# A hand-written schedule in another order behind its 199th step (routing attention, then a SiLU layer, one core)

## The chip, the cores and the metric

The kernel runs on one core of a Trainium2 chip. The metric is the device time of one execution in microseconds (us), lower is better. Three runs of the kernel before gave 294.0, 295.02 and 587.43 us, so their median is 295.02; the third is twice the other two and says nothing about the kernel's work. A fourth execution, taken with the profiler, gave 293.75 us.

The engines are named as in the profile: PE multiplies matrices (PEld is its loading of weights), ACT is the scalar engine, DVE the vector engine, POOL the third engine for elementwise work, and SP only issues transfers. Each takes its instructions strictly in the order in which they stand in its own queue, and waits at the first one whose inputs are not there.

## The reference

Shapes: q, k and v are [4, 8, 768, 64] (batch, heads, sequence, head width), there are 16 centroids per head, w_in is 512 x 2048 and w_out 2048 x 512. All are float32.

```
q_assign = argmax(q_n . c_n);  k_assign = argmax(k_n . c_n)        # cluster of each row, 16 per head
scores = where(q_assign == k_assign, (q . k^T) / sqrt(64), -1e9)
attn = softmax(scores);  x = attn . v                              # -> [3072, 512]
h = x @ w_in;  out = (h * sigmoid(h)) @ w_out
```

## The kernel before

The kernel has no loop over its work. A table of 1628 words, `plan`, is read from front to back, and each word emits one step through `step(op, n, eng, banks)`. The letters say what the step does, the number says which head, unit or tile, a letter behind the point chooses the engine of a copy (A is ACT, D is DVE, P is POOL), and digits there choose PSUM banks. The pools hand out buffers in the order of the steps, and the semaphores follow from that. So the table alone sets the order on all five queues.

There are 32 heads in all (4 batches of 8). A head n passes through these steps:

- `r` loads q and k (L92, on SP); `hi` and `lo` split float32 into two float16 halves (L103/L105/L107 by engine, and L112 on DVE). The `hl` tile that they fill is one of four, so `hi` also waits until an earlier head's tile has been read.
- `ht` turns the tile by a DMA transpose into `ab` (L121, on SP). Heads 0 to 7 do this on PE instead.
- `l` multiplies `ab` with the centroids on PE (L159, 12 matmuls of 32 columns). `ls`, `mx`, `ge` (DVE) make the cluster's one-hot rows of it.
- The one-hot rows are written into partitions 64 to 79 of `ab`, for the mask is part of the score's matmul. Heads 8 to 15: `cm` on PE, `ce` (L237 on ACT or L239 on DVE), and a transfer on SP (L240). Heads 16 to 31: `cs` on POOL (L204, L205), `cx`, a DMA transpose on SP (L213), and `cv`, a transfer on POOL's queue (L217).
- `qk` makes two score tiles of 384 columns on PE (L336) in one of two double banks, `ex` their exponentials on ACT (L341), `pv` multiplies them with v (36 matmuls of 65 columns, L353), `nm` normalises (DVE, L363, L365). `pt` and `pe` (PE, then a copy) or `xd` (L392, a DMA transpose on SP) turn the result into `xt`. `vl` loads v, `v` casts it (L277 on ACT, L279 on DVE or POOL).

The layer behind it: for batches 0 and 1 `a` and `e` multiply with w_in (L401), `t` is the tanh (ACT, L413) and `g` the gate (DVE, L416). For batches 2 and 3 `y` (L467), `u` and `s` do the same with fewer products. The second matrix is `b` (L498) for three row tiles, and `m` (L559) with its sums `S` (DVE, L572) and copies `z`, `o` (L587, L581, L590) for the rest. The weights come in through twelve transfers on POOL's queue: `w0` to `w7` w_in (L608, 256 KB each), `w8` to `w11` w_out (L611, 512 KB each). Each stands behind a copy of one element (`pace`, L604) that reads the newest exponential tile, which holds it back until that exponential is done.

Every transfer of SP stands in one queue, whatever it is for, and an SP transfer that must wait holds all behind it.

Of the kernel before, what the change touches and what calls it, by code (L numbers as in the profile page):

```python
# [29 lines left out]
def kernel(  # L30
# [655 lines left out]
    def step(op, n, eng, banks):  # L686
# [138 lines left out]
        ex19 qk21 xL1.2 ex20 w8 xM1 ex21 qk22 qk23 pt2.0 ex22 ex23 xm1 px3.1 qk24 pe0.D lo8 xg1 xc1 py3 qk25 ex24 qk26  # L825
        pe2.D a1.0 xe1.A nm3 pt3.1 pe3.D a0.2 ex25 ex26 qk27 ex27 e1 e4.1 e0 t4 g4 vl10 qk28 t0 g0 qk29 ex28 e6.3 t6
        g6 ex29 vl11.P e3.1 t3 w9 t1 e5.2 qk30 ex30 w11 g3 lo9 r13 vl8 qk31 t5 pv4.3 qk32 ex31 nm4 e8.1 g1 g5 qk33 ht8
        lo10 hi11.P e14.0 ex32 ex33 t14 g14 qk34 t8 ex34 qk35 e11.2 e13.3 ht10 g8 wc4 wc5 t11 g11 r12 ex35 t13 g13
        qk36 ex36 e10.1 e15.0 qk37 pt4.2 qk38 e2.3 t10 ex37 ex38 lo11 pe4.D ht9 r14 pv5.2 g10 t15 nm5 qk39 qk40 t2
        ex39 ex40 e7.1 e12.2 t12 ht11 g15 qk41 ex41 t7 g2 r15 wc6 e9.0 qk44 g7 t9 g9 pv6.3 nm6 wc0 wc8 ex44 qk42 ex42  # L830
        b0.1 pt5.0 v11.P l8.3 ls8 mx8 hi13.P ge8 lo13 qk43 qk45 pe5.A b4.0 ex43 qk47 wc12 wc1 cm8.3 b1 ex45 g12 ce8.A
        qk46 ex46 l10.3 b5 ls10 mx10 l9.2 ls9 ht13 mx9 b6 b7 od1 ex47 ge9 cm9.3 hi12.A lo12 ce9.A bo1 pv7.2 nm7 hi14.A
        b2 pt6.3 pt7.0 pe7.A ht12 r16 ge10 lo14 l11.2 ls11 ht14 mx11 b3 cm10.0 bo0 ce10.D pe6.A e25.3 t25 qk50 ex50
        ge11 g25 qk48 hi15.D e27.2 cm11.1 t27 g27 ce11.A e20.0 t20 lo15 ex48 qk49 g20 e17.3 t17 l12.1 hi16.P ex49 vl13
        e23.2 qk52 ls12 mx12 l13.0 ls13 g17 ex52 t23 g23 vl9 e31.1 t31 od2 qk75 e28.0 ex75 v8.P t28 g31 e18.3 t18 mx13
        qk51 ex51 qk53 v10.A e24.2 t24 ge12 g18 g28 l14.1 ls14 mx14 e22.3 qk59 ge13 ex53 cm12.0 ex59 ht15 r18 e29.1
        t29 qk54 ex54 ce12.D g24 cm13.0 ce13.D g29 t22 g22 qk55 ex55 lo16 ge14 e19.2 t19 g19 v9.A e16.0 e30.1 t16 g16
        qk57 r17 t30 qk56 e21.3 t21 m1.2 ex56 g30 wc15 wc13 r19 g21 ht16 l15.0 ls15 ex57 S3 pv8.1 vl17 qk58 nm8 cm14.3
# [15 lines left out]
        ex101 vl23 e63.0 S21 qk124 ex124 e53.3 qk105 t53 g53 e51.2 t51 v18.A g51 pv16.1 nm16 e55.3 cs23 ex105 cv22
        qk128 t63 ex128 g63 v19.A m22.2 qk130 ex130 vl21 S22 m21.1 z20.A v23.P o20 qk109 ex109 qk110 ex110 vl28 v22.A
        m26 qk108 ex108 l24.0 hi27.D lo27 ht27 cx23 pv17.2 z21.D ls24 qk113 mx24 qk112 t55 v21.P l26.0 g55 ex113 m25
        nm17 ls26 mx26 r28 cv23 ex112 xd16 xd17 qk111 ex111 qk131 ex131 e57.3 t57 e52.2 v28.A z22.D S24 qk126 ex126
        m27.0 qk127 g57 pv18.3 o23 r30 hi25.D lo25 nm18 qk115 ht25 ex127 qk116 m24 o22 ex115 ex116 qk114 ex114 xd18
# [69 lines left out]
```

## Time and profile before

| | |
|---|---|
| three runs | 294.0, 295.02, 587.43 us |
| the profiled execution | 293.75 us, of which the span of its instructions is 292.0 us |
| PE | 284.4 us busy, 97% |
| ACT | 244.5 us, 84% |
| DVE | 228.3 us, 78% |
| POOL | 66.7 us, 23% |
| granted TensorE clock | full in every slice |

Times in the profile are microseconds from the span's start. A row of instructions gives the engine, the line of the kernel, the operation, output and input names, shapes, how many, and then the busy time and the mean of one in nanoseconds; behind it stands how long the engine was idle before them and who ended that. A row of the timeline gives start, duration, engine, line and, in brackets, idle time and its releaser; rows of equal neighbours are merged, so their duration can hold a gap. Matmuls are pipelined: a row's matmuls start closer together than the mean of one says.

### The profile page before, as it was taken

How to read it: one execution, taken by the hardware profiler on the slowest of the kernel's cores; microseconds unless marked ns; L12 is line 12 of the kernel's file. 1: busy time of each engine (PE TensorE's matmuls, PEld its weight loads, DVE VectorE, ACT ScalarE, POOL GpSimd, SP SyncE). 2: the span in 40 equal slices, each digit the busy share in tenths (PEclk: the TensorE clock that was granted, in tenths of full speed). 3: DMA queues.
4: the chain of work that ended last, by engine and by line, in shares of the span. 5: the costliest groups of instructions: out<-in, count | busy, mean ns of one | idle time of the engine just before them, and what ended most of it. 6: DMA issues, size and time to landing. Idle time of an engine off the chain costs nothing.

```text
span 292.0 us, 8452 instructions
## 1 busy us (share of the span) xinstructions
PE 284.4 (97%) x3356; PEld 208.4 (71%) x3356; DVE 228.3 (78%) x498; ACT 244.5 (84%) x427; POOL 66.7 (23%) x114
## 2 busy tenths in 40 slices
PE   7899999999999999999999999999999999999995
PEld 3767766756678886776777788765687878656884
DVE  5898949699999999878788899888944623897662
ACT  5898999976989999988999998879899989486631
POOL 2654905110400015552232042111220000000000
PEclk9999999999999999999999999999999999999999
DMA  7999999999898888999778796392000222210032
GB/s 209 288 274 237 188 182 198 206 229 210 217 221 178 194 193 177 202 199 231 190 118 193 193 190 123 77 245 85 18 24 2 88 43 76 74 38 2 2 124 92
DMA packets 75750, 44.01 MB, mean 151 GB/s; under 512 B 53872, under 2 KB 72080, under 8 KB 75712
## 3 DMA queue, kind: packets, MB, share of 16 engines
q1 hardware_dynamic: 71584, 38.01, 55.9%
q0 software_dynamic: 3840, 5.18, 10.5%
q8 instruction: 26, 0.43, 0.6%
q10 hardware_dynamic: 288, 0.30, 0.4%
q14 instruction: 12, 0.10, 0.1%
HBM read 27.30 MB, written 6.29 MB: 115 GB/s over the span
## 4 chain that ended last, share of the span: by engine, by line
PE 87%; DVE 4%; DMA 3%; ACT 3%; issue 1%; SPq 0%; DVEq 0%; ACTq 0%
PE pS L336 20%; PE xb L559 18%; PE ph L401 14%; PE pO L353 11%; PE gd L467 5%; PE psN L159 4%; PE yb L559 3%; PE gx L467 3%; PE po L498 2%; PE gy L467 2%; DMA xt<-xn 2%; DMA raw<-in_q_dram 1%; PE wb L559 1%; ACT P L341 1%; DVE hl L112 1%
## 5 line engine op out<-in xcount | busy, mean ns | idle before, releaser
L341 ACT ACTIVATE P<-pS 128x768 f16<-128x768 f32 x192 | 149.7, 816 | 10.1 <-PE pS L336 8.4
L336 PE MATMUL pS<-ab 128*128 128x384 f16 x384 | 86.8, 326 | 0.3 <-ACT P L341 0.2
L401 PE MATMUL ph<-xt,win_s 128*128 128x384 f16 x256 | 49.7, 326 | 0.5 <-DMA xt<-xn 0.4
L336 PEld LDWEIGHTS <-ab 128*128 128x128 f16 x384 | 33.8, 98 | 15.1 <-issue 1.8
L353 PEld LDWEIGHTS <-P 128*128 128x128 f16 x1152 | 39.7, 97 | 3.8 <-DVE cd L239 0.4
L416 DVE SCALAR_TENSOR_TENSOR gt<-tn,ph 128x384 f16<-128x384 f32 x64 | 33.6, 548 | 10.6 <-ACT tn L413 10.3
L353 PE MATMUL pO<-vt,P 128*128 128x65 f16 x1152 | 41.3, 193 | 0.0
L559 PEld LDWEIGHTS <-gt 128*128 128x128 f16 x352 | 34.2, 98 | 7.2
L401 PEld LDWEIGHTS <-win_s 128*128 128x128 f16 x256 | 24.4, 98 | 16.0 <-issue 0.9
L413 ACT ACTIVATE tn<-ph 128x384 f32<-128x384 f32 x64 | 30.6, 507 | 3.8 <-PE ph L401 3.2
L112 DVE SCALAR_TENSOR_TENSOR hl<-raw,hl 128x768 f16<-128x768 f32 (+3 forms) x35 | 31.8, 912 | 0.2
L559 PEld LDWEIGHTS <-s 128*128 128x128 f16 x264 | 25.7, 98 | 5.3
L105 POOL TENSOR_SCALAR hl<-raw 128x768 f16<-128x768 f32 (+1 forms) x10 | 20.2, 2016 | 28.2 <-DMA raw<-in_k_dram 15.1
L559 PE MATMUL xb<-wout_s,gt 128*128 128x256 f16 x176 | 22.6, 273 | 0.0
L159 PEld LDWEIGHTS <-ab 128*128 128x128 f16 x496 | 18.0, 97 | 4.0 <-DVE ab L146 0.4
L559 PE MATMUL xb<-wc,s 128*128 128x256 f16 x160 | 20.7, 273 | 0.0
L204 POOL TENSOR_SCALAR od<-od 128x96 f16<-128x96 f16 x16 | 9.6, 599 | 48.3 <-DVE od L197 45.6
L581 ACT ACTIVATE ot<-xb 128x256 f32<-128x256 f32 x33 | 12.8, 387 | 8.6 <-PE xb L559 8.4
L159 PE MATMUL psN<-stk,ab 128*128 128x32 f16 (+1 forms) x496 | 19.1, 186 | 0.0
L572 DVE TENSOR_TENSOR s<-gt 128x1024 f16<-128x1024 f16 x22 | 15.3, 694 | 4.7 <-PE xb L559 3.8
L365 DVE TENSOR_TENSOR xn<-pO,zr 128x384 f16<-128x384 f32 x32 | 17.8, 558 | 1.1
L467 PEld LDWEIGHTS <-win_s 128*128 128x128 f16 x128 | 12.3, 98 | 8.5 <-issue 0.8
(128 smaller groups left out, 412.5 us busy)
## 6 DMA issues: line engine op xcount, KB each, us to landing
raw<-in_k_dram SPq DMA_DIRECT2D x31, 192.0 KB, 3.7
vn<-in_v_dram SPq DMA_DIRECT2D x31, 192.0 KB, 3.7
raw<-in_q_dram SPq DMA_DIRECT2D x24, 192.0 KB, 3.7
out_dram<-ot SPq DMA_DIRECT2D x18, 256.0 KB, 2.7
win_s<-in_moe_w_in_dram POOLq DMA_DIRECT2D x8, 256.0 KB, 6.9
wout_s<-in_moe_w_out_dram POOLq DMA_DIRECT2D x4, 512.0 KB, 9.2
out_dram<-ot SPq DMA_DIRECT2D x12, 128.0 KB, 1.7
raw<-in_q_dram SPq DMA_DIRECT2D x2, 384.0 KB, 5.9
```

Of the source, the lines that this page charges most:

```text
L105: nc.gpsimd.tensor_scalar(out=o, in0=i, scalar1=QS, scalar2=None, op0=ALU.mult)
L112: nc.vector.scalar_tensor_tensor(out=hl[:, s, 1, :], in0=raws[job.name][:, s, :], scalar=QS, in1=hl[:, s, 0, :], op0=ALU.mult, op1=ALU.sub ...
L159: nc.tensor.matmul(L[:, n % 2, :, n // 2], ab[:, i, :], stk[:, job.groups[i // 3][0], x : x + w], start=(x == 0), stop=(x + w == 2 * HC),)
L336: nc.tensor.matmul(pS[:, e, 0:HALF], abs_[kj.name][:, kn, :], rhs, start=True, stop=True)
L341: nc.scalar.activation(out=P, in_=pst.pop(u)[:, :, 0:HALF], func=AF.Exp, bias=0.0, scale=ESC)
L353: nc.tensor.matmul(o[:, (2 * t + h) * VW : (2 * t + h + 1) * VW], Ps[i + h, c, j // 2][:, j % 2, ts(t, 128)], vtb[(i + h) % 13][:, j, 0:VW ...
L365: nc.vector.tensor_tensor(out=xn, in0=ov[:, :, 0:D], in1=zr.unsqueeze(2).to_broadcast([128, 2 * NM, D]), op=ALU.mult)
L401: nc.tensor.matmul(ph[:, 0:HALF], win_s[:, r, ts(fb, 128)], xts[b, c][:, r, :], start=(r == 0), stop=(r == NR - 1))
L413: nc.scalar.activation(out=tn, in_=phs[b, c, fb][:, 0:HALF], func=AF.Tanh, bias=0.0, scale=0.5)
L416: nc.vector.scalar_tensor_tensor(out=gt[:, fb, NM * c : NM * c + NM, :].rearrange("p t n -> p (t n)"), in0=tns.pop((b, c, fb)), scalar=1.0 ...
L467: nc.tensor.matmul(o[:, 0:HALF], w[:, r, :], x[:, r, :], start=(s in (7, 1) and r == 0), stop=(r == 1), skip_group_check=True)
L559: nc.tensor.matmul(o, self.lhs(l, f), self.rhs(r, f), start=(f == 0 and opens), stop=(f == HB - 1), skip_group_check=True)
```

## The change

The table keeps its 1628 steps, and each step keeps what it computes. The first 199 words stay. From the 200th on the words stand in another order, many with other bank digits, and some copies with another engine letter. Among the first 450 steps the transfers keep the order that they had among themselves. The engine letters move this work, counted over the whole program: on ACT three fewer `hi`, seven fewer casts of v and one fewer copy to `xt`, six more copies in the products' mixes (L481) and one more of the cluster rows; on DVE six fewer copies in the mixes (L479) and one fewer of the cluster rows, three more casts, one more `hi` and one more copy to `xt`; on POOL two more `hi` and four more casts.

```diff
@@ -822,74 +822,74 @@
-        ex19 qk21 xL1.2 ex20 w8 xM1 ex21 qk22 qk23 pt2.0 ex22 ex23 xm1 px3.1 qk24 pe0.D lo8 xg1 xc1 py3 qk25 ex24 qk26
...
+        ex19 qk21 ex20 xL1.1 qk23 xM1 xm1 pt2.2 pe2.D ex21 qk22 px3.0 xg1 ex23 ex22 qk27 ex27 xc1 qk25 ex25 lo9 py3
...
```

Three places follow. The first is on PE, at the centroid product of head 8 (the first `psN` of 32 columns; `ab_1221` there and `ab_1293` now are that head's transposed tile). The rows of before, of which repeats are left out:

```order
L498 LDWEIGHTS gt_95
L498 MATMUL po_1463<-wout_s_67,gt_95 128x512
L374 LDWEIGHTS xn_1360
L374 MATMUL px_1468<-ident_84,xn_1360 128x128
L159 LDWEIGHTS ab_1221
L159 MATMUL psN_1473<-stk_68,ab_1221 128x32
```

And the rows now:

```order
L353 LDWEIGHTS P_1217
L353 MATMUL pO_1303<-vt3_73,P_1217 128x65
L159 LDWEIGHTS ab_1293
L159 MATMUL psN_1344<-stk_68,ab_1293 128x32
L336 LDWEIGHTS ab_426
L336 MATMUL pS_1357<-ab_877,ab_426 128x384
```

It stood as PE's row 1564 and stands as row 1422 now: 71 matmuls that were ahead of it are behind it. By kind they are 16 of L401, 4 of L498, 36 of L353, 12 of L336 and 3 of L374.

The second place is POOL around the last three of w_out's transfers. Before, from the 43rd row of its queue:

```order
L743 MEMSET od_92 128x256
L604 COPY pace<-P 1x1
L611 DMA wout_s<-in_moe_w_out_dram 128x4x512
L271 DMA vn<-in_v_dram 128x384
L604 COPY pace<-P 1x1
L611 DMA wout_s<-in_moe_w_out_dram 128x4x512
L604 COPY pace<-P 1x1
L611 DMA wout_s<-in_moe_w_out_dram 128x4x512
L105 TENSOR_SCALAR hl<-raw 128x12x64
L279 CAST vt_81<-vn 128x6x64
```

And now:

```order
L743 MEMSET od_92 128x256
L604 COPY pace<-P 1x1
L611 DMA wout_s<-in_moe_w_out_dram 128x4x512
L105 TENSOR_SCALAR hl<-raw 128x12x64
L271 DMA vn<-in_v_dram 128x384
L604 COPY pace<-P 1x1
L611 DMA wout_s<-in_moe_w_out_dram 128x4x512
L604 COPY pace<-P 1x1
L611 DMA wout_s<-in_moe_w_out_dram 128x4x512
L743 MEMSET od_94 128x256
```

The three are w8, w9 and w11. Head 11's `hi` moved ahead of v's load and of w9 and w11. Each `pace` copy reads another exponential than before: in the table w8 stands behind ex24 (it stood behind ex20), w9 behind ex26 (ex29, but with more of PE's work ahead of it now) and w11 behind ex33 (ex30).

The third place is DVE, where the second halves of heads 8 and 9 are made (`hl_853` is head 8's tile, `hl_940` head 9's; `cd` are the cluster rows of the pair x1). Before:

```order
L112 SCALAR_TENSOR_TENSOR hl_853<-raw_213,hl_853 128x12x64
L197 TENSOR_TENSOR om0_89<-psN_965,mxn_1010 128x192
L385 COPY xt_942<-px_1002 128x384
L363 RECIPROCAL zr_1073<-pO_1012 128x6
L365 TENSOR_TENSOR xn_1075<-pO_1012,zr_1073 128x384
L385 COPY xt_942<-px_1077 128x384
L416 SCALAR_TENSOR_TENSOR gt_95<-tn_1102,ph_1096 128x384
```

And now:

```order
L197 TENSOR_TENSOR om0_89<-psN_967,mxn_995 128x192
L112 SCALAR_TENSOR_TENSOR hl_940<-raw_589,hl_940 128x12x64
L239 TENSOR_SCALAR cd_1069<-psN_967 96x256
L385 COPY xt_942<-px_826 128x384
L363 RECIPROCAL zr_1082<-pO_1007 128x6
L365 TENSOR_TENSOR xn_1084<-pO_1007,zr_1082 128x384
L112 SCALAR_TENSOR_TENSOR hl_853<-raw_213,hl_853 128x12x64
```

Head 9's second half, which stood behind four gates, moved ahead of head 8's, and the copy of x1's cluster rows came from ACT to DVE. On SP the order from here is the same as before for twelve more transfers: head 13's load, a load of v, the transposes of heads 8 and 10, head 12's load, head 9's transpose, head 14's load, head 11's transpose, head 15's load. (A load is two transfers.)

More of the change, by code (lines that the diff above doesn't have):

```diff
@@ L829 @@
[L829 to L838, printed above, removed]
@@ L854 @@
[L854 to L858, printed above, removed]
@@ L889 @@
-        y312 y283 u292 y295 y294 s300 s310 u302 y305 y304 s302 s261 u312 y315 u303 s303 S83 u293 s292 y314 u313 s312
-        S81 y303 s301 S82 m81.3 m87 y313 m91.2 z80.A y293 m86 s311 s313 s281 m92.1 S84 s293 s291 z81.D S93 S91 m85
-        z82.D o83 m97 S92 m82.0 o80 m84 o82 z90.A m96 z91.A S103 o90 m83 m95 o81.A z92.A S94 m101.0 z100.D S101 S102
-        m93 o91.D m106 z101.A m107.1 o93 m105 z102.A S104 o103 m94 o92 m103 o101.D m104 o102 m102.3 o100
+        ex19 qk21 ex20 xL1.1 qk23 xM1 xm1 pt2.2 pe2.D ex21 qk22 px3.0 xg1 ex23 ex22 qk27 ex27 xc1 qk25 ex25 lo9 py3
@@ new lines @@
+        qk24 ex24 w8 xe1.D pe0.D a0.2 qk31 ex31 nm3 pt3.1 a1.3 lo8 vl10 qk34 pe3.D e4.0 e0 ex34 t4 g4 e1 t1 qk29 qk28
+        t0 g0 g1 e6.1 ex29 ex28 t6 hi11.P g6 e2.0 e7.2 t7 g7 e3.3 t2 g2 vl11.P qk26 qk35 e5.1 ex26 pv4.2 w9 t3 g3 ex35
+        lo10 e13.0 t5 qk32 e9.3 t13 nm4 ex32 v10.D g5 pt4.2 pe4.D qk30 ex30 qk33 ex33 lo11 w11 e8.1 g13 r13 e12.2 t8
+        g8 wc0 t12 g12 t9 g9 qk39 vl8 ht8 ht10 ex39 od2 qk41 pv5.0 nm5 l8.1 qk37 ls8 ex41 ex37 e11.2 t11 g11 wc1 e15.3
+        t15 qk44 ex44 e10.0 qk36 mx8 ge8 l10.1 ls10 qk38 g15 mx10 r12 t10 ht9 g10 ex36 wc2 e14.2 t14 ex38 hi13.P b4.1
@@ new lines @@
+        qk42 b5 hi12.D lo13 r14 qk43 ht11 r15 ex42 g14 qk40 v8.P ex40 pt5.3 pe5.D wc8 cm8.0 ce8.D ex43 b6 l9.2 ht13
+        pv6.3 ls9 mx9 ge9 qk46 ex46 b7 cm9.0 nm6 ce9.A lo12 qk47 ex47 pt6.2 l11.3 bo1 ls11 ge10 ht12 qk45 r16 mx11
+        ge11 b0.0 b1 ex45 pe6.A hi14.D lo14 pv7.1 ht14 nm7 cm10.3 ce10.A cm11.2 ce11.A vl13 qk50 qk48 ex48 hi15.D lo15
+        wc4 wc9 b2 b3 bo0 pt7.3 ex50 l13.2 ls13 pe7.A ht15 e25.1 t25 mx13 g25 e28.3 t28 g28 ge13 e31.0 t31 g31 vl14
+        e17.2 t17 g17 e20.1 l12.3 ls12 mx12 t20 g20 vl9 qk52 ex52 e23.0 cm13.2 ce13.A t23 wc12 ge12 e24.3 t24 g23 qk75
@@ new lines @@
+        pv17.1 qk111 hi27.D lo27 ht27 vl23 e58.2 v21.P hi25.A cv22 ex111 cv23 qk115 e52.0 ex115 m26 t52 S24 nm17 z21.D
+        xd17 qk113 ex113 g52 e49.1 qk131 t49 v20.P lo25 l26.0 ex131 ls26 qk112 ex112 g49 m25 v22.P l24.0 z22.D r30 t58
+        g58 ls24 qk114 pv18.1 nm18 qk127 ex114 mx24 qk126 ex127 m23 mx26 ht25 ex126 qk116 ex116 vl31 hi28.P lo28 e56.2
+        qk117 ex117 r31 m27.0 qk118 o23 qk119 ex118 ge24 cs24 ex119 cx24 e53.1 ws13 m24 o22 ge26 qk123 o21.A ex123 t53
+        r29 g53 v23.P pv19.3 nm19 t56 g56 qk138 ex138 qk121 e48.0 ex121 l25.1 qk125 xd19 ls25 ex125 mx25 ge25 e61.3
@@ L893 @@
+        m97 o83 z90.A m84 m96 z91.A o82 m83 S94 S103 m95 o81.A m92.1 z92.D m101.3 m93 S101 S102 z100.D m106 z101.D
+        m107.2 m105 o90 S104 o91.D o93 z102.D o103 m94 o92 m103 m104 o101.A o102 m102.1 o100
     """.split()
```

98 lines of the change are left out of this document (50 added, 48 removed).

## The prediction

> **What bounds the kernel now.** I read the page first, then the table of stretches, then who waited for whom, and last the timelines of SP, POOL and PE between 38 and 69 us, where the first steps in another order meet the transfers.
>
> ```profile
> span 292.0 us, 8452 instructions
> PE 284.4 (97%) x3356; PEld 208.4 (71%) x3356; DVE 228.3 (78%) x498; ACT 244.5 (84%) x427; POOL 66.7 (23%) x114
> ...
> 20.00:40.00 20.00, 19.29 (x339) 14.47 (x338) 16.89 (x38) 18.05 (x26) 11.60 (x23) 1.00 1.01 202
> 120.00:140.00 20.00, 19.58 (x217) 13.56 (x215) 16.56 (x36) 17.74 (x32) 8.07 (x10) 1.00 1.06 207
> 240.00:260.00 20.00, 19.81 (x223) 13.97 (x221) 13.60 (x30) 14.68 (x27) 0.00 (x0) 1.00 0.20 62
> 280.00:292.00 12.00, 8.66 (x80) 7.51 (x77) 4.66 (x9) 2.64 (x7) 0.00 (x0) 1.00 0.30 100
> ```
>
> PE bounds it. The columns of the stretches are length, then busy time of PE, PEld, DVE, ACT, POOL, then clock, share of the transfer engines, GB/s. PE lacks 0.42 us between 120 and 140, 0.19 between 240 and 260, and less elsewhere between 40 and 280; the 3.34 us after 280 are the last tile's way out. As its 3356 matmuls stay the same, another order can only remove or add waits of PE. 2% of the median is 5.9 us, about what a measurement of this kernel can tell from no change. Between 20 and 280 us there is far less than that to remove, so a gain of over 2% needs a shorter start or end, and the first 199 words and the last product (`m102`, `o100`) stand where they stood.
>
> So the question is which new wait of PE the order makes. The transfers are the place to look, since the table orders PE, DVE and ACT freely but a transfer takes what the engines' load leaves:
>
> ```profile
> 38.00:42.00 4.00, 4.00 (x29) 2.48 (x27) 1.69 (x4) 3.65 (x7) 0.00 (x0) 1.00 1.07 159
> 54.00:58.00 4.00, 4.00 (x56) 2.83 (x55) 2.49 (x7) 3.89 (x7) 0.53 (x1) 1.00 1.21 206
> ...
> 38.73 0.62 SPq L271 DMA_DIRECT2D vn<-in_v_dram  x1
> 45.20 0.33 SPq L92 DMA_DIRECT2D raw<-in_q_dram  x1
> 47.41 1.63 SPq L121 DMA_TRANSPOSE ab<-hl  x1
> 49.13 7.56 SPq L121 DMA_TRANSPOSE ab<-hl  x1
> 57.90 2.34 SPq L121 DMA_TRANSPOSE ab<-hl  x1
> 61.48 2.17 SPq L121 DMA_TRANSPOSE ab<-hl  x1
> ...
> 43.93 0.75 POOL L611 DMA_DIRECT2D wout_s<-in_moe_w_out_dram  x1 [0.29 <-issue]
> 45.76 0.75 POOL L611 DMA_DIRECT2D wout_s<-in_moe_w_out_dram  x1 [0.55 <-DMA vn<-in_v_dram]
> 57.47 2.13 POOL L105 TENSOR_SCALAR hl<-raw 128x768 f16<-128x768 f32 x1 [8.35 <-DMA ab<-hl]
> ...
> DMA to landing us min/median/max: 3.7/4.6/11.1
> ```
>
> The transfer engines are full there (share 1.07 to 1.21), at some 200 GB/s. The SP rows are a load of v, head 13's load (45.20), then the transposes of heads 8, 10, 9 and 11. POOL's `hi` of head 13 takes head 8's tile and was released at 57.4, so head 8's transpose landed 10 us after its issue, behind w9 (43.93) and w11 (45.76). Head 10's issue was itself held 7.56 us; as the longest it landed at 49.13 + 11.1 = 60.2. Heads 9 and 11, with the median of 4.6, landed at about 62.5 and 66.1. These tiles are read by the centroid products:
>
> ```profile
> 58.96 0.51 PE L159 MATMUL psN<-stk,ab 128*128 128x32 f16 x12
> 62.45 0.51 PE L159 MATMUL psN<-stk,ab 128*128 128x32 f16 x12
> 63.66 0.51 PE L159 MATMUL psN<-stk,ab 128*128 128x32 f16 x12
> 68.22 0.51 PE L159 MATMUL psN<-stk,ab 128*128 128x32 f16 x12
> ```
>
> Heads 8, 10, 9 and 11 in this order: 1.6, 2.2, 1.2 and 2.1 us behind their landings. The old order was fitted to these landings with little to spare.
>
> **The change part by part.** *The four products move ahead.* PE's time for a kind, from pieces of the chain in which nothing waits:
>
> ```profile
> 41.44 1.95 PE ph L401 x12
> 43.39 0.65 PE pS L336 x4
> 44.04 1.09 PE pO L353 x36
> 64.18 1.73 PE po L498 x8
> ```
>
> That is 0.1625 us for a matmul of L401 or L336, 0.030 for L353, 0.216 for L498. Head 8's product now has 16 L401 (2.60), 4 L498 (0.86), 36 L353 (1.09), 12 L336 (1.95) and 3 transposes (about 0.17) fewer ahead of it: 6.7 us. It would stand at 58.96 - 6.7 = 52.3. Counted in the same way head 10's comes 6.9 us earlier (55.6), head 9's 2.9 (60.7), head 11's 4.2 (64.0). If the transposes landed as before, PE would wait 57.4 - 52.3 = 5.1 us at head 8; the others need 4.6, 1.8 and 2.1, which that one wait covers. So this term lies between 0 and 5.1 us.
>
> *What moves the landings.* Before, SP stood idle from 39.35 to 45.20:
>
> ```profile
> SPq L92 <- DVE zr L363: 6.0, 1, 6.0
> ```
>
> This is head 13's load waiting for the buffer of head 9, that is for head 9's second half on DVE, the row ahead of the named one. That half now stands ahead of head 8's on DVE, and x1's cluster rows come sooner too. So SP can go on at about 39.4, and head 13's load, v's load and head 8's transpose are issued by about 42, not 49. On POOL w9 has (by the table's count of PE work ahead) 4.0 us more of PE's work ahead of the exponential that it waits for, and w11 5.5: they go out at about 47.9 and 51.3. For head 8's transpose both weights, 512 KB each or 2.6 us at 200 GB/s, thus move from ahead to behind: 57.4 - 5.2 = 52.2, and its product stands at 52.3: no wait. For head 10's, which waits for its own second half on DVE (where it was: about 48), only w11 moves behind: 60.2 - 2.6 = 57.6 against 55.6, 2.0 us; with both behind it, 0. For heads 9 and 11 the same transfers as before are ahead, and engines that were full cannot do them sooner: 1.8 and 2.1 us. One wait of PE covers the later ones, so about 2 us in all; the share of 1.00 to 1.1 before 46 us leaves perhaps 0.5 us of room. I take 1.5, nearer to 0 than to 5.1, because it follows from sums of bytes that reproduce the old landings.
>
> *Head 12's split comes to DVE.* `hi12` left ACT for DVE and waits there for head 12's load (issued at 57.37 before, landed at about 61) with head 13's second half and the gates queued behind. DVE comes to it some 7 us behind head 8's product, at about 59 plus that wait. It may stand 1 us; the products that read the gates behind it come over 3 us later on PE, so nothing is added. Without that cover it costs 1.
>
> *A wait that goes.*
>
> ```profile
> 130.07 5.21 DMA xt<-xn
> ...
> 134.42 0.49 PE L401 MATMUL ph<-xt,win_s 128*128 128x384 f16 x2
> 135.33 0.48 PE L401 MATMUL ph<-xt,win_s 128*128 128x384 f16 x2 [0.42 <-DMA xt<-xn]
> ```
>
> Batch 1's second half began with a wait for a transpose: 135.33 - 134.42 less two matmuls (0.33) is 0.58 us. The table now puts 8.3 us of PE work between this transpose and the first product that reads it (4.7 before). Next late is the transpose issued behind it, with 6.4 us of PE work; the chain's first row gives 5.21 from issue to landing, so it is in time by about 1. I take -0.6.
>
> *Copies on other engines.* ACT loses eleven ops and gains seven, DVE loses two in all, POOL gains six. None of the three bounds the kernel as a whole (84%, 78% and 23% busy), so I count 0. The price if this is wrong comes from these rows:
>
> ```profile
> L105 POOL TENSOR_SCALAR hl<-raw 128x768 f16<-128x768 f32 x7 | 15.0, 2137 | 23.5 <-DMA raw<-in_k_dram 15.1 <-DMA ab<-hl 8.3
> L279 POOL CAST vt<-vn 128x384 f16<-128x384 f32 x16 | 9.9, 631 | 16.1 <-DMA vn<-in_v_dram 15.6 <-DMA raw<-in_k_dram 0.6
> L107 DVE TENSOR_SCALAR hl<-raw x14: 549/553/1619, 7.1 to 174.4; 128x768 f16<-128x768 f32 x13, 128x576 f16<-128x576 f32 x1
> L112 DVE SCALAR_TENSOR_TENSOR hl<-raw,hl x35: 353/948/1380, 4.0 to 177.4; 128x768 f16<-128x768 f32 x26, 128x576 f16<-128x576 f32 x7, 128x384 f16<-128x384 f32 x1, 128x192 f16<-128x192 f32 x1
> ```
>
> POOL gets 2 x 2.14 + 4 x 0.63 = 6.8 us more. The last two rows give shortest, median and longest: some DVE ops took up to 1.07 us more than their like.
>
> *Everything else behind 69 us.* New short waits may come, such as `v23` on POOL, which now stands right ahead of the `pv` that reads it. One cast is 0.63 us; half of that is 0.3.
>
> Sum: 293.75 + 1.5 - 0.6 + 0.3 = 294.95 for an execution like the profiled one. Of the four executions three lie close together, 293.75, 294.0 and 295.02; their middle is 0.25 above the profiled one, so 295.2.
>
> **The rivals.** *A: the transfers get ahead, PE waits nowhere new.* If head 10's transpose also passes w9, and heads 9's and 11's pass w11, the 1.5 falls away, and some of the short waits after 200 us too (0.3): 294.0 - 0.6 - 0.3 = 293.1. For it speaks SP's idle 5.85 us; against it that the engines were full.
>
> *B: the transposes land no sooner than before.* They did not pass the weights in the old trace. If w8, which now goes out later too, fills the engines, head 8's product waits the whole 5.1: 294.0 + 5.1 - 0.6 + 0.3 = 298.8.
>
> *C: POOL holds DVE up, and PE waits for DVE.* From 60 to 80 us DVE has nothing to spare:
>
> ```profile
> 60.00:80.00 20.00, 20.00 (x214) 12.67 (x213) 19.43 (x40) 15.61 (x28) 2.98 (x4) 1.00 1.01 233
> ```
>
> It is busy 19.43 of 20 us, so from there on a DVE op that is held goes on to PE as soon as a gate or a sum is the last thing that a product waits for. If each of POOL's six added ops held such an op for its whole length, it would cost 6.8 us: 294.0 + 1.2 + 6.8 = 302.0. The rows of L107 and L112 show that DVE ops are held at times; against it stand the largest excess of 1.07 us, that most of POOL's added ops come behind 90 us, where DVE has more room, and DVE's own 1.7 us less.
>
> The Trainium skill has a rule for this ("SBUF — State Buffer", section "Who interferes with whom"): DVE and GpSimd, the profile's POOL, take a shared port pair for a whole instruction, and the second to start waits for the first to end, if DVE's runs in a two-port mode or reads two operands from SBUF. By that rule the price of C is right for every DVE op of such a kind that starts just behind one of POOL's. The trace agrees in kind, with 1619 ns against a median of 553 for an op of L107, but in no row with a hold of 2.14.
>
> **How the numbers follow.** My forecast, about 1.5 us of wait at the four products, 295.2: 0.5. A, 293.1: 0.27. B, 298.8: 0.15. C, 302.0: 0.08. The range that leaves out no more than 2 in 10 runs from just under A, 292.4 (A less the 0.7 by which those three executions lie about the middle of their extremes), to just over B, 299.2; C and the edges are left out. Faster by over 2% would be below 289.1, which no case reaches: 0.02 for what I do not see. Slower by over 2%, above 300.9, is C and a little of B with further waits: 0.10. Within 2%: 0.88.
>
> **What would show it.** Right: head 13's load leaves SP about 6 us sooner, head 8's transpose is issued by 42 and lands at 51 to 53; the four rows of L159 stand at 52 to 66 with PE waits of 1 to 2 us on `ab<-hl` in all; the wait on `xt<-xn` at 135 is gone; POOL is busy about 6.8 us more and DVE and ACT a little less, with PE's waits for them as small as before. A is seen by no wait on `ab<-hl`. B is seen by a landing of head 8's transpose near 57, C by rows of L112 or L572 over 2 us and PE waits on DVE. I am wrong altogether if PE waits over a microsecond somewhere behind 140 us, for one of `cv`'s transfers or one of the late loads of v, since I have costed those at 0.3 in all.

## The result, and the profile after

The changed kernel takes 306.28 us (median of four executions, 305.71 to 307.46) against 294.96 for the kernel before: a ratio of 1.040, 95% interval 1.036 to 1.043. It is slower by 4%, above the upper end of the forecast's range (299.2). The profiled execution took 306.64 us, its span 304.9, which is 12.9 more than before. Some of the kernels below have executions in two groups some 7 us apart; where the median would hide that, both are given.

The page of the changed kernel:

```profile
span 304.9 us, 8457 instructions
PE 288.1 (94%) x3356; PEld 209.6 (69%) x3356; DVE 226.0 (74%) x496; ACT 241.8 (79%) x423; POOL 71.4 (23%) x120
...
PEclk9999999769999999999999999999999999999999
```

PE is busy 3.7 us more with the same 3356 matmuls, and two slices show less than the full clock. Who PE waited for:

```profile
PE psN L159 <- DMA ab<-hl: 9.0, 3, 3.6
```

Columns: total, times, longest. The wait for `xt<-xn` is gone; three waits of the centroid products for transposed tiles are new. PE's rows of them, for heads 8, 10 and 22:

```profile
55.86 0.55 PE L159 MATMUL psN<-stk,ab 128*128 128x32 f16 x12 [3.61 <-DMA ab<-hl]
64.36 0.82 PE L159 MATMUL psN<-stk,ab 128*128 128x32 f16 x12 [3.38 <-DMA ab<-hl]
...
135.86 0.52 PE L159 MATMUL psN<-stk,ab 128*128 128x32 f16 x12 [2.02 <-DMA ab<-hl]
```

And PE by stretches cut at the changes of its clock (columns as in the prediction: the clock is the third from the end):

```profile
50.00:52.00 2.00, 2.00 (x42) 1.60 (x40) 1.55 (x4) 2.00 (x5) 1.16 (x3) 1.00 1.28 125
52.00:55.80 3.80, 0.24 (x8) 0.12 (x4) 1.32 (x4) 0.98 (x2) 0.09 (x1) 1.00 1.33 105
56.30:59.60 3.30, 3.30 (x14) 1.57 (x11) 1.27 (x3) 1.30 (x2) 2.25 (x2) 0.50 1.21 193
59.70:63.00 3.30, 1.28 (x8) 0.57 (x6) 0.84 (x3) 2.30 (x4) 0.00 (x0) 1.00 1.41 122
63.10:69.80 6.70, 5.44 (x26) 2.71 (x27) 4.02 (x8) 1.50 (x3) 0.00 (x0) 0.50 1.13 302
70.00:72.00 2.00, 2.00 (x15) 1.15 (x14) 0.56 (x2) 1.02 (x3) 0.00 (x0) 1.00 0.00 0
```

Behind each of the first two waits PE runs at half its clock, about 3.4 us the first time and 6.8 the second (of which it works 5.5, from 64.36 on). Half of 3.4 and of 5.5 is 4.45 us lost. The account closes: 9.0 of waits + 4.45 of clock - 0.6 for the wait that went = 12.85, against 12.9 in the span. It says where the time lies, not what each part would give back alone: the first 1.7 of the clock passes while head 10's tile is still on its way, and at full clock PE would have waited that much longer there.

Why the tiles were late begins on POOL. Its queue before, then now (w8, a load of v, w9, w11; the copy at 39.38 is w8's `pace`):

```profile
35.26 0.75 POOL L611 DMA_DIRECT2D wout_s<-in_moe_w_out_dram  x1
36.00 0.55 POOL L271 DMA_DIRECT2D vn<-in_v_dram  x1
```

```profile
39.38 0.37 POOL L604 COPY pace<-P 1x1 f16<-1x1 f16 x1 [3.98 <-ACT P L341]
39.84 0.75 POOL L611 DMA_DIRECT2D wout_s<-in_moe_w_out_dram  x1
40.62 2.15 POOL L105 TENSOR_SCALAR hl<-raw 128x768 f16<-128x768 f32 x1
42.70 0.59 POOL L271 DMA_DIRECT2D vn<-in_v_dram  x1
...
46.49 0.78 POOL L611 DMA_DIRECT2D wout_s<-in_moe_w_out_dram  x1 [0.64 <-issue]
51.02 0.75 POOL L611 DMA_DIRECT2D wout_s<-in_moe_w_out_dram  x1 [0.28 <-issue]
```

w8 goes out 4.6 us later and the load of v 6.7 us later than before. SP on the other hand runs ahead, as forecast: head 13's load is issued at 38.98 (45.20 before) and head 8's transpose at 40.76. From issue to landing the transposes of heads 8 and 10 took (last column, us, of the table of transfers, for the stretches 40.5 to 41 and 47 to 48):

```profile
ab<-hl SPq DMA_TRANSPOSE x1, 15.0
...
ab<-hl SPq DMA_TRANSPOSE x1, 16.9
```

Head 8's needed 9.9 before (47 to 48):

```profile
ab<-hl SPq DMA_TRANSPOSE x1, 9.9
```

Issued 6.6 us sooner, it landed 1.5 us sooner (55.8), and head 10's landed at 64.3, four us later than before.

### The profile page after: what moved, and what is told of

Same layout as the page of the kernel before. It is cut to its first block, busy times and chain, and to the rows that moved or that the text cites. A ratio compares the mean times of both kernels' runs of the same rounds, so it can differ in the third digit from the quotient of the medians.

```text
span 304.9 us, 8457 instructions
## 1 busy us (share of the span) xinstructions
PE 288.1 (94%) x3356; PEld 209.6 (69%) x3356; DVE 226.0 (74%) x496; ACT 241.8 (79%) x423; POOL 71.4 (23%) x120
## 4 chain that ended last, share of the span: by engine, by line
PE 81%; DMA 10%; DVE 3%; ACT 3%; issue 1%; POOL 0%; DVEq 0%
PE pS L336 18%; PE xb L559 17%; PE ph L401 12%; PE pO L353 10%; DMA ab<-hl 8%; PE gd L467 5%; PE psN L159 4%; PE yb L559 3%; PE gx L467 3%; PE po L498 3%; PE gy L467 2%; ACT P L341 2%; DMA ab<-cd 2%; PE wb L559 1%; DMA craw<-in_centroids_dram 1%
## 5 line engine op out<-in xcount | busy, mean ns | idle before, releaser
L336 PE MATMUL pS<-ab 128*128 128x384 f16 x384 | 87.2, 329 | 0.7 <-DMA ab<-cd 0.3
L401 PE MATMUL ph<-xt,win_s 128*128 128x384 f16 x256 | 51.7, 336 | 0.0
L336 PEld LDWEIGHTS <-ab 128*128 128x128 f16 x384 | 33.7, 98 | 15.4 <-issue 2.3
L353 PEld LDWEIGHTS <-P 128*128 128x128 f16 x1152 | 39.6, 97 | 4.1 <-DVE cd L239 0.4
L353 PE MATMUL pO<-vt,P 128*128 128x65 f16 x1152 | 41.1, 193 | 0.0
L401 PEld LDWEIGHTS <-win_s 128*128 128x128 f16 x256 | 25.3, 100 | 16.7 <-issue 2.0
L105 POOL TENSOR_SCALAR hl<-raw 128x768 f16<-128x768 f32 (+1 forms) x12 | 24.2, 2020 | 12.0 <-DMA raw<-in_q_dram 5.4
L168 DVE TENSOR_REDUCE L<-psN 128x192 f32<-128x384 f32 x24 | 13.2, 552 | 12.9 <-PE psN L159 12.7
L279 POOL CAST vt<-vn 128x384 f16<-128x384 f32 x20 | 12.6, 643 | 40.7 <-DMA vn<-in_v_dram 40.5
L204 POOL TENSOR_SCALAR od<-od 128x96 f16<-128x96 f16 x16 | 8.8, 551 | 55.4 <-DVE od L197 55.4
```

The source lines that it names most:

```text
L105: nc.gpsimd.tensor_scalar(out=o, in0=i, scalar1=QS, scalar2=None, op0=ALU.mult)
L336: nc.tensor.matmul(pS[:, e, 0:HALF], abs_[kj.name][:, kn, :], rhs, start=True, stop=True)
L353: nc.tensor.matmul(o[:, (2 * t + h) * VW : (2 * t + h + 1) * VW], Ps[i + h, c, j // 2][:, j % 2, ts(t, 128)], vtb[(i + h) % 13][:, j, 0:VW ...
L401: nc.tensor.matmul(ph[:, 0:HALF], win_s[:, r, ts(fb, 128)], xts[b, c][:, r, :], start=(r == 0), stop=(r == NR - 1))
```

## The experiments

Behind each time stand in brackets its ratio to the kernel before, timed beside it, and the 95% interval of the ratio. In the cuts from the table, words left out are marked by dots.

**Idle PE loses its clock.** Theory: the half clock follows from the waits. Rival: it has another cause. The words `j16` and `j22` put in 16 and 22 products of zeros, which PE works on while it would wait.

```diff
- ... od2 qk41 pv5.0 nm5 l8.1 ... mx8 ge8 l10.1 ls10 ...
+ ... od2 qk41 pv5.0 nm5 j16.1 l8.1 ... mx8 ge8 j22.1 l10.1 ls10 ...
```

> The changed kernel with PE kept busy during its two long waits: 16 products of zeros (512 columns, 0.216 us each, so 3.45 us) stand right ahead of head 8's centroid product and 22 (4.74 us) right ahead of head 10's. Theory (the two half-clock stretches, 56.2 to 59.6 and 63.1 to 69.9, follow from PE standing idle ahead of them): the clock is 1.00 from 50 to 72 us; the tiles land no sooner, so head 8's product starts at 55.9 as before; PE comes to head 10's 1.7 us sooner and still starts it at 64.4; the second stretch's 5.5 us at half rate (2.8 us lost) go: 306.3 - 2.8 = 303.5. Rival (the clock falls for another reason, such as how full the transfer engines are): it still reads about 0.5 behind 56 and 63, and the time stays at 306.3 or above.

302.8 us (1.028, 1.024 to 1.032). The same stretches, and the rows of the fillers:

```profile
56.30:59.60 3.30, 3.30 (x21) 1.86 (x20) 2.16 (x5) 2.92 (x6) 1.02 (x2) 1.00 1.24 188
...
63.10:69.80 6.70, 6.64 (x69) 3.93 (x68) 5.16 (x12) 3.51 (x5) 0.00 (x0) 1.00 0.96 265
```

```profile
52.02 3.62 PE L620 MATMUL junk<-zz 128*128 128x512 f16 x16
55.70 0.51 PE L159 MATMUL psN<-stk,ab 128*128 128x32 f16 x12
58.97 4.91 PE L620 MATMUL junk<-zz 128*128 128x512 f16 x22
63.94 0.51 PE L159 MATMUL psN<-stk,ab 128*128 128x32 f16 x12
```

The clock stays full and the two products start within 0.2 and 0.4 us of where they did: the tiles' landings, not PE, set those. From head 10's product to head 9's PE needs 5.16 us (63.94 to 69.10), where it needed 7.86 at half clock (64.36 to 72.22): 2.7 us are the clock, where 2.8 were expected. In this execution the third wait was short too (0.3 us instead of 2.0); with the 0.4 us by which head 10's tile came sooner that makes up the 4.7 us between the spans (304.9 and 300.2), to 0.1.

The Trainium skill has the rule ("TensorE: Matmul & The Clock Gate", Part 1): PE's clock falls to half behind an idle stretch of about 3.4 us, and rises after as long of activity, on a grid of 3413 ns that runs on its own. The trace agrees in the size (3.41 and 6.83 us at half rate) and in the grid: read in stretches of 0.2 us, the clock changed at 56.23, 59.64, 63.06 and 69.88 us, whole multiples of 3.41 us apart. But a stretch that was idle only in part was enough: the two ahead of the half clock were idle for 3.0 and 2.1 us of 3.41, and the one from 63.06 on, idle for 1.3, left the clock at half for another.

**One product moved in the kernel before.** Do the products alone do it?

```diff
- ... nm5 qk39 qk40 ... v11.P l8.3 ls8 mx8 hi13.P ...
+ ... nm5 qk39 l8.2 ls8 qk40 ... v11.P mx8 hi13.P ...
```

> The kernel before with one step moved: head 8's centroid product and its sum stand 5.3 us of PE work earlier (in bank 2, behind qk39, so at about 53.6), all transfers as they were. Theory (an earlier product finds a transpose that lands no sooner, and idle PE loses its clock besides): PE waits 3.7 us until the landing at 57.3, and if most of one stretch of 3.4 us falls into the wait, another 1.7 us go at half clock: 294.7 + 3.7 = 298.4, or 300.1 with the clock. Rival (the waits of the changed kernel come of its other moves, and this one is covered): no wait over 1 us, 294.7 to 295.7.

300.77 us (1.019, 1.013 to 1.025), with a single new wait:

```profile
57.30 0.52 PE L159 MATMUL psN<-stk,ab 128*128 128x32 f16 x12 [3.26 <-DMA ab<-hl]
```

The clock was at half from 58.6 to 62.1. The theory is right to 0.7 us: here a product moved ahead of its transpose costs the wait, and about half as much again in clock (1.7 us on 3.3).

**What holds the transposes.** POOL's transfers against SP's own.

```diff
+        elif n in (9, 11):
+            nc.gpsimd.memset(wout_s[:, 4 * (n - 8) : 4 * (n - 8) + 4, :], 0.0)
```

> The changed kernel without the transfers w9 and w11 (1 MB of the 2 MB of w_out); POOL writes zeros into their place instead, so the output leaves half of w_out out. Theory (w9 and w11 in POOL's queue hold the transposes of heads 8 and 10 back): head 8's transpose shares the engines only with w8 and a load of v and lands by 52.5, head 10's by 54.5; the products start at 52 and 55.5 with less than 0.5 us of wait, the clock stays at 1.00, and 3.8 + 3.5 + 4.5 us go: 306.3 - 11.8 = 294.5, with the third wait (2.2 us at 136) left. Rival (SP's own transfers that now stand ahead, head 13's load and a load of v, hold them): head 8's still lands at about 55 and head 10's behind 60: 303 to 306.

299.13 us (1.011, 1.007 to 1.015), between the theory (294.5) and the rival (303 and more). Head 10's transpose came at 56.1 instead of 64.3 (the theory had 54.5); head 8's at 54.8, where the theory had 52.5 and the rival 55. Its product still waited 2.2 us, and the clock fell behind that:

```profile
54.88 0.52 PE L159 MATMUL psN<-stk,ab 128*128 128x32 f16 x12 [2.20 <-DMA ab<-hl]
```

So in this order w9 and w11 hold head 10's transpose, and something else most of head 8's. The next kernel also moves the load of v:

```diff
  (as the one before, and)
- ... g2 vl11.P qk26 ...  qk40 v8.P ex40 ...
+ ... g2 qk26 ...  qk40 v8.P vl11.P ex40 ...
```

> As the run without w9 and w11 (zeros in their place, so half of w_out is left out), and the load of v for head 11 on POOL's queue is moved back behind the cast of head 8's v, so that of POOL's transfers only w8 is left while heads 8's and 10's transposes are in flight. Theory (the transposes share the engines turn by turn with whatever POOL's queue holds, and get through when it is empty): w8 lands by about 48, head 8's transpose by 50.5, head 10's by 52; PE waits for neither, the clock stays at 1.00, and beside that run's 299.1 the 2.2 us at head 8 and the 1.7 us at half rate go: about 295, with 0 to 2 us left at head 22. Rival (head 8's transpose is slow by itself, or for what SP holds ahead of it): it lands at 53 to 55 again and the time stays at 298 to 300.

296.14 us (1.004, 1.000 to 1.008). Head 8's transpose landed at 52.1, head 10's at 53.4; neither product waited and the clock stayed full.

```profile
52.74 0.52 PE L159 MATMUL psN<-stk,ab 128*128 128x32 f16 x12
56.02 0.51 PE L159 MATMUL psN<-stk,ab 128*128 128x32 f16 x12
```

The theory's landings were 1.5 us too early, its time 1 us too low (1.2 us of wait at head 22 are in it). So the load of v on POOL's queue counts too: with it later, both transposes land 2.7 us sooner.

**Packets of half the size.**

```diff
-            nc.gpsimd.dma_start(wout_s[:, 4 * r : 4 * r + 4, :], ...)
+            for h in (slice(0, DH), slice(DH, DM)):
+                nc.gpsimd.dma_start(wout_s[:, 4 * r : 4 * r + 4, h], ...)
```

> The changed kernel with each of w_out's four transfers made as two of half the columns: the same bytes in the same place, in packets of 512 B instead of 1024 B. Theory (the engines take turns packet by packet between SP's queue and POOL's, so a transpose's 256 B packet waits out one of POOL's packets, some 97 ns, each time): with packets of about 55 ns a turn is some 86 ns instead of 128, head 8's transpose lands at about 52.4 instead of 55.8, head 10's at about 60.7 instead of 64.3; PE waits 0.3 and 4.8 instead of 3.8 and 3.5, and one stretch at half clock goes: about 302. Rival (a transpose waits for the bytes issued ahead of it, whatever their packets): both land where they did, 306.3. Second rival: the weights come so much later that the second product (row tiles b5, b7) waits for them instead: 306 or above with waits of PE on w_out.

304.42 us (1.035, 1.030 to 1.039), 2.4 above the theory's forecast. The table of queues (packets, MB, share of 16 engines; q1 is SP's, q0 POOL's) between 56 and 60 us, of the changed kernel and of this one:

```profile
q0 software_dynamic: 614, 0.61, 91.0%
q1 hardware_dynamic: 608, 0.16, 30.4%
```

```profile
q0 software_dynamic: 708, 0.35, 77.9%
q1 hardware_dynamic: 920, 0.24, 66.8%
```

In this stretch of the changed kernel both queues get the same number of packets, and each of SP's (256 B of a transpose) stands against one of POOL's (1 KB). In the kernel before SP's queue moved 2196 packets in the 2 us behind 56, when POOL's was empty:

```profile
q1 hardware_dynamic: 2196, 0.55, 126.3%
```

That is about seven times as many per us. With packets of half the size SP's number rose from 608 to 920, in the direction that the theory had. But the turns were no longer even (708 to 920), a packet of POOL's took 70 ns (77.9% of 16 engines' 4 us, over 708) where the theory had 55, and one of SP's 46 instead of 32, and the landings moved less (head 8's to 53.5, head 10's to 63.1). The Trainium skill gives the rule ("DMA: Bandwidth & Descriptors", section "Queues, rings and completion order"): each transfer engine goes round the queues for which it has work, packet by packet. 614 to 608 agrees, but other stretches do not. Between 48 and 52 us of the changed kernel, with w9 and head 8's transpose both in flight, SP's queue moved 929 packets and POOL's 83; without w9 and w11 it was 641 and 34, and the two together only 64 GB/s. So equal turns are shown for one stretch, and what slows head 8's transpose ahead of it is not.

**w9, w11 and the load of v later.**

```diff
- ... g2 vl11.P ... pv4.2 w9 ... lo11 w11 ... ex41 ex37 e11.2 ... qk40 v8.P ex40 ...
+ ... g2 ... pv4.2 ... lo11 w9 ... ex41 ex37 w11 e11.2 ... qk40 v8.P vl11.P ex40 ...
```

> The changed kernel, complete, with three of POOL's transfers later: w9 stands where w11 stood (behind ex33), w11 behind ex37, and head 11's load of v behind the cast of head 8's v. The order on PE, DVE, ACT and SP stays. Theory: w9 is issued at about 50 and w11 at 53.5; head 8's transpose has the engines with w8 alone and lands by 51, head 10's by 54 to 55; w9 lands by 57 and w11 by 60, ahead of the products that read them (58 and 63); PE waits less than 1 us at heads 8 and 10, the clock stays at 1.00: 306.3 - 11.8 = 294.5, up to 2 less if the third wait stays away too. Rival (there are more bytes than the stretch can carry, so something else comes late): PE waits 2 us or more for w9 or w11, or for the gates behind the sums on DVE that read them: 297 to 301.

305.13 us (1.031, 1.024 to 1.037): the rival was right in kind, and its 297 to 301 too low. Heads 8's and 10's transposes landed at 52.2 and 53.5 and their products did not wait, but two later things did:

```profile
62.37 1.02 PE L498 MATMUL po<-wout_s,gt 128*128 128x512 f16 x4 [3.02 <-DMA wout_s<-in_moe_w_out_dram]
...
69.68 0.52 PE L159 MATMUL psN<-stk,ab 128*128 128x32 f16 x12 [2.83 <-DMA ab<-hl]
```

Now w9, w11 and head 9's transpose are in flight together, and the transfers fell to a quarter of their rate (last column, GB/s, at a full share; 201 between 56 and 58 us):

```profile
60.00:62.00 2.00, 0.00 (x0) 0.00 (x0) 0.00 (x0) 0.20 (x1) 0.00 (x0) 1.00 1.19 49
62.00:64.00 2.00, 1.63 (x7) 0.78 (x7) 1.35 (x3) 0.00 (x0) 0.00 (x0) 0.83 1.38 53
```

The same with the third wait taken on:

```diff
  (as the one before, and)
- ... e39.0 l20.1 r24 qk86 ls20 t39 ht22 e45.2 ...
+ ... e39.0 l20.1 qk86 ls20 t39 ht22 r24 e45.2 ...
```

> The run before it and, on SP, head 22's transpose ahead of head 24's load. Theory: all three waits of the changed kernel are gone and its own gain is left (no wait for the normalised tile at 135, 0.6 us): 293.0 to 294.0, a little below the kernel before. Rival (a later load of head 24 makes another late, or the weights do): as the run before it or above, 294.5 to 300.

296.33 us in the profiled execution and 302.76 to 304.05 in the five others, so its median says little. In the profiled one head 9's transpose landed in 6.6 us, ahead of w9, where it took 17.1 in the run before; that part of the two programs is the same. What decides it stays open.

**The third wait alone.** The edit just shown, on the changed kernel.

> The changed kernel with head 22's transpose ahead of head 24's load (384 KB) on SP, nothing else. Theory (the third wait, 2.2 us at 135.9, is this transpose's late issue at 129.3 and the load's packets ahead of it): it is issued at 127.9 and lands by 132.5 instead of 135.8, PE does not wait for it: 306.3 - 2.2 = 304.1. Rival (the full engines make it late wherever it stands, 6.5 us from issue to landing): it lands at 134.4 or later, PE still waits 0.7 us or more: 304.8 to 306.3.

302.94 us (1.027, 1.021 to 1.033). The wait at head 22 is gone. That is 2.0 us; the profiled execution (301.85) is shorter by more, but that lies ahead of the steps that were moved, which run behind 120 us: its first wait was 2.6 us, and its second, 3.5 us, lay so across the clock's grid (1.7 us of it ahead of the edge at 62.0, 1.8 behind) that no half clock followed.

**Which steps.** The tables cut at the 445th step and joined both ways.

> The other way round: the changed kernel's first 445 steps, then the rest in the order of before. Theory: both waits of 3.5 us and the half clock behind them stay, the third wait does not come: 306.3 - 2.2 + 0.6 = 304.7, between 302 and 306. Rival: under 298, if the loss belongs to the later steps.

306.92 us (1.036, 1.028 to 1.044), waits of 3.70 and 2.25 us at heads 8 and 10: the first 445 steps are enough for the loss. The other way round:

> The kernel before in its first 445 steps (up to some 76 us), then the steps that are left, in the changed kernel's order with its banks and engine letters. Theory (the loss is made in the first 450 steps, by heads 8's and 10's products against their transposes and by the clock behind those waits): no wait over 0.5 us at heads 8 to 11, clock 1.00 throughout, the wait for the normalised tile at 135 gone (0.6), head 22's wait 0 to 2.2: 294.1 to 296.3. Rival (the order behind the 445th step costs by itself): above 297.5, with new waits of PE between 80 and 280 us.

299.89 us (1.017, 1.013 to 1.021), over the range of the theory and in that of the rival. The products of heads 8 to 11 do not wait; but the joint itself made a wait on DVE, and a half clock behind it, which neither kernel has:

```profile
79.93 0.31 PE L226 MATMUL psC<-ident,om 128*96 128x128 f16 x2 [2.37 <-DVE om L197]
```

Head 22's wait was 1.9 us. With head 24's load behind that transpose:

> The run before it with head 22's transpose ahead of head 24's load. Theory: the third wait goes as well: 293.5 to 294.5, level with the kernel before or up to 0.4% below it. Rival (head 24's load is then the late one, or the wait was not always there): as the run before it within its interval.

299.25 us (1.014, 1.010 to 1.018): head 22's wait went, the joint's stayed. With the joint mended (`mx13 ge13` ahead of two gates, `v10 wc2 wc9` behind `ce13`, one product ahead of `cm13`):

> The kernel before in its first 447 steps, then the rest in the changed kernel's order, with head 22's transpose ahead of head 24's load, and the seam at 78 us mended: there head 13's maximum and cluster rows come ahead of two gates and of the cast and the two w_out combinations that had piled up on DVE, and one product of w_in comes ahead of head 13's rows on PE. Theory: no wait of PE over 1 us is left between 40 and 280 us and the clock stays at 1.00: 293.2 to 294.8. Rival (a further cost in the later steps that the two runs with the seam hid): 296 or above.

297.03 us (1.011, 1.009 to 1.013), in the rival's range. But from 76 to 81 us PE idles 1.6 us, at the joint, in short waits for DVE and ACT, and behind it no wait is over 0.2 us: between 81 and 280 us PE idles 0.5 us, in the kernel before 0.9. So nothing speaks for a cost of the order behind the 447th step.

**POOL's two early transfers.** What the profile after suggested: put w8 and the load of v back.

```diff
- ... ex19 qk21 ex20 xL1.1 ... qk24 ex24 w8 xe1.D ... lo8 vl10 qk34 ... g2 vl11.P qk26 ...
+ ... ex19 qk21 ex20 w8 xL1.1 ... qk24 ex24 xe1.D ... lo8 vl10 vl11.P qk34 ... g2 qk26 ...
```

> The changed kernel with w8 back behind ex20 and head 11's load of v back ahead of head 11's first half on POOL, so that these two go out at about 35.5 and 37 as in the kernel before, not at 39.8 and 42.7. Theory one (the later start of w8 and of this load made head 8's transpose late): w8 and the load land by 47, head 8's transpose by 52.5, and the wait at head 8 falls under 0.7 us; head 10's stays late behind w9 and w11 (62 to 64): about 302. Theory two (whatever POOL's queue holds beside a transpose holds it up, and w9 and w11 take the place of the two): head 8's lands at 54 to 57.5 again, and the time stays at 304 to 307.

296.81 us (1.010, 1.007 to 1.013): 9.5 of the 11.3 us come back with two words. Theory one was right for head 8. For head 10 it was not: with w9 and w11 where they were, its transpose was to stay late (62 to 64), and it did not. The landing times of heads 8's and 10's transposes (stretches 41.2 to 42 and 47.5 to 49), and PE's products of heads 8, 10 and 9:

```profile
ab<-hl SPq DMA_TRANSPOSE x1, 10.6
...
ab<-hl SPq DMA_TRANSPOSE x1, 8.2
```

```profile
52.57 0.51 PE L159 MATMUL psN<-stk,ab 128*128 128x32 f16 x12
56.10 0.52 PE L159 MATMUL psN<-stk,ab 128*128 128x32 f16 x12
62.44 0.52 PE L159 MATMUL psN<-stk,ab 128*128 128x32 f16 x12 [1.00 <-DMA ab<-hl]
```

Head 8's lands at 51.9 and head 10's at 56.1, though w9 and w11 still go out at 47.0 and 51.5. SP issues head 8's transpose as early as in the changed kernel (41.28), so its early issue is not what made it late there. One word each:

> The changed kernel with w8 alone back behind ex20, so issued at about 35; head 11's load of v stays behind head 11's first half on POOL, at about 42. Theory (both late starts count; the load of v beside a transpose costs it 2.7 us, as the two runs without w9 and w11 showed): head 8's transpose lands at 53 to 54.5, PE waits 1 to 2 us at head 8, and little at head 10: 297.5 to 300. Rival (w8 is all of it): as the run with both back, 296.8.

297.28 us (1.006, 1.004 to 1.009); eight of ten executions lie at 295.1 to 297.7, two at 299.8 and 305.4. The rival (296.8) was nearer than the theory (297.5 to 300, with 1 to 2 us of wait at head 8), for that wait is gone:

```profile
52.97 0.52 PE L159 MATMUL psN<-stk,ab 128*128 128x32 f16 x12
```

POOL's rows tell why: the load of v was held by the copy ahead of w8, which waited for ex24; with ex20 it goes out at 38.85 without being moved.

```profile
35.99 0.75 POOL L611 DMA_DIRECT2D wout_s<-in_moe_w_out_dram  x1
36.76 2.15 POOL L105 TENSOR_SCALAR hl<-raw 128x768 f16<-128x768 f32 x1
38.85 0.59 POOL L271 DMA_DIRECT2D vn<-in_v_dram  x1
```

> The changed kernel with head 11's load of v alone back ahead of head 11's first half on POOL; w8 stays behind ex24, at 39.8. Theory: the load follows w8 in POOL's queue and goes out only 2 us sooner, beside the same transpose: head 8's lands at 54 to 56 and PE still waits over 1.5 us at head 8 and 2 us at head 10: 301 to 306. Rival (the load of v is all of it): 297 to 298.

297.95 us in the profiled execution (waits of 0.5 and 0.7 us at heads 10 and 9), 302.69, 306.24 and 306.82 in the others: three of four at or a little above the theory's 301 to 306. What those three waited for was not seen.

**A repaired version.** Both words back, head 22's transpose ahead of head 24's load, and

```diff
- ... b6 l9.2 ht13 pv6.3 ls9 ... b7 cm9.0 nm6 ce9.A lo12 qk47 ex47 pt6.2 ...
+ ... b6 ht13 pv6.3 l9.2 ls9 ... b7 nm6 lo12 qk47 ex47 cm9.0 ce9.A pt6.2 ...
```

> The run with w8 and head 11's load of v back (296.8), with its two last waits taken on: head 22's transpose ahead of head 24's load (2.2 us), and head 9's product behind the 36 products of pv6 instead of ahead of them, with head 9's cluster rows behind the score of qk47 (1.2 us). Theory: 296.8 - 2.2 - 1.2 = 293.4, from 293.0 to 294.4, which is level with the kernel before (294.1 to 294.8 in these series) or a little below it. Rival (something later comes in the place of the two): 295.5 or above.

294.93 us beside 295.03 for the kernel before: 1.001, 0.998 to 1.003 (one of twelve executions at 304.55). The waits at heads 8, 9, 10 and 22 are gone or under 0.3 us; two of 0.4 and 0.5 us for DVE came in. With these taken on as well (`hi12.D` moved back to `lo12`, `nm6` ahead of `ls9`; the combination of w_out that the expectation names kept its place):

> The run level with the kernel before (294.9), with the two waits of PE taken on that its own moves had made on DVE (0.5 us each at 61 and 65): head 12's first half and one combination of w_out come later on DVE, behind head 9's rows, and pv6's normalisation ahead of head 9's sum. Theory: 294.9 - 1.0 = 293.9, from 293.2 to 294.5, about 0.3% below the kernel before and hardly to be told from it. Rival (head 12's transpose is then late for its own product, or DVE stays the limit there): 294.7 or above.

294.79 beside 294.36: 1.003, 1.000 to 1.006. The forecast was 0.9 too low, and the rival's range (294.7 or above) holds it. By stretches, of the kernel before and of this one:

```profile
0.00:40.00 40.00, 36.71 (x576) 26.07 (x577) 32.37 (x91) 34.08 (x54) 21.72 (x44) 1.00 0.96 232
120.00:280.00 160.00, 159.10 (x1754) 118.03 (x1752) 119.10 (x251) 135.54 (x244) 27.04 (x45) 1.00 0.49 108
```

```profile
0.00:40.00 40.00, 36.25 (x572) 25.97 (x573) 33.23 (x92) 33.95 (x53) 23.80 (x45) 1.00 0.94 232
120.00:280.00 160.00, 159.60 (x1783) 118.38 (x1781) 116.70 (x244) 137.86 (x248) 32.69 (x51) 1.00 0.48 109
```

Between 120 and 280 us PE idles 0.5 us less than before, the wait at 135 that went; ahead of 40 us it idles 0.46 more. So the new order, repaired, is level with the old one, and no version was found that beats both.

## Why the prediction was wrong, point by point

*That PE bounds the kernel, that the four centroid products are the place, and that they would stand at 52.3 and 55.6*: right. PE came to head 8's at 52.2 (55.86 less the wait of 3.61) and, at full clock (the run with fillers), to head 10's 3.3 us behind head 8's, as worked out.

*SP goes on at 39.4 instead of 45.2 and head 8's transpose is issued by 42*: right (38.98, 40.76).

*"For head 8's transpose both weights ... move from ahead to behind"*: this step failed. w9 and w11 did go out at 46.5 and 51.0, near the 47.9 and 51.3 worked out. But the sum left w8 and head 11's load of v where they had been, though both had moved on POOL's queue; they went out at 39.8 and 42.7, just ahead of head 8's transpose (40.76) and just behind it, so two others took the place of w9 and w11. With w8 put back alone the wait at head 8 went and 9 us came back. With both back head 8's transpose landed at 51.9, for which the sum had 52.2, and head 10's at 56.1, for which it had 57.6. The sum came out for an order that the kernel did not have, and in part by luck, for its rule was wrong as well: that a transfer is either ahead of another or behind it. What is issued behind still slows a transpose: in the run without w9 and w11 the load of v goes out at 43.15, behind head 8's (40.80), and with that load out of the way as well head 8's landed at 52.1 instead of 54.8. And with w8 still late, but w9, w11 and the load of v away, head 8's landed at 52.1 too. By what steps the transfers hold each other up is shown only in part (equal turns in one stretch) and stays open.

*"this term lies between 0 and 5.1 us", since one wait covers the later ones*: wrong at the upper end. It took the old landings as the latest possible; head 10's landed 4.1 us later than before, and the two waits are 3.61 + 3.38 = 7.0 us.

*Rival B* named the right cause (w8 goes out later and fills the engines) and got 0.15; its price of 5.1 had the same bound.

*Missing altogether: the clock.* That another order "can only remove or add waits of PE" was wrong: the matmuls themselves took longer. Each wait was priced by its length, and 4.45 us of half clock came on top. The fillers gave 2.7 of these back; the other 1.7 would have turned into a longer wait at head 10. One stretch of half clock is 1.7 us, and with it rival B would have come out beyond the range (300.5).

*The wait that goes at 135 (-0.6)*: right.

*Everything else behind 69 us, 0.3*: wrong by 2 us, at head 22's transpose. The condition named (a wait of over a microsecond behind 140 us, for `cv` or a load of v) had the kind of wait right and neither the tile nor the place: it is the same product and kind of transpose as at heads 8 and 10, behind another load on SP.

*Copies on other engines, head 12's split on DVE*: right at 0; behind 10 us PE waits for DVE nowhere over 0.4 us, so rival C did not happen. POOL is busy 4.7 us more, where 6.8 was worked out; nothing hung on it.

With what was measured put into its sum, 293.75 + 7.0 + 2.0 + 4.45 - 0.6 = 306.6, the profiled execution's 306.64.

## What to carry to other kernels

Where transfers fill their engines, go down every queue that feeds them and note for each transfer, not only for the ones that the change is about, which wait now stands ahead of it: here one word that made a copy on POOL wait 4 us for a later exponential cost 9 us of the kernel's time in most executions. Price a transfer's landing by all that is in flight beside it, not only by what was issued ahead of it, and do not take its old landing as a bound. Price a wait of TensorE of some 2 us or more with the half clock that can follow it, and see in the clock by stretches whether it did.

## What the runs showed of the hardware that was not expected

Whether half clock follows a wait depends on where the wait lies. The stretches at half clock were 3.41 us long, or 6.83, and their ends give the grid of each execution. Where it could be read, what counted was how long PE was idle within one stretch of that grid. With 2.1 us or more at full clock, half clock followed: 2.1 in the kernel before with one product moved and ahead of the changed kernel's second half clock, 2.2 in the run without w9 and w11, 3.0 ahead of the changed kernel's first. With 1.8 us or less at full clock it did not: the 3.5 us of the run with head 22's transpose first were 1.7 and 1.8 in two stretches, and the 2.0 us at head 22 of the changed kernel 0.9 and 1.1.

A DMA transpose of the same size took from 4.0 us (head 11's in the changed kernel, behind the last weight) to 17.1 us (head 9's beside w9 and w11 in the run with these later) from issue to landing. Beside weights the two queues moved equal numbers of packets in one stretch (614 and 608) and very unequal ones in another (83 and 929); in a third the transfers fell to about 50 GB/s together, and the same program fell into one course or the other from execution to execution (296.3 and 303 to 304). Why is open.
